# Sparse attention and MLP on one core: engine order from a list scheduler, scores in row halves, batch 1's row sums from row reads

## The chip, the cores and the metric

One core of one Trainium2 chip runs the whole program. The metric is the device time of one execution in microseconds (us). Before the change its median is 319.44 us over three runs (318.63 to 320.3).

Engines: TensorE (PE) multiplies matrices; its weight loads are listed as PEld and run beside its matmuls. VectorE (DVE), ScalarE (ACT) and GpSimd (POOL) do elementwise work; SyncE (SP) issues transfers, and so does POOL. PE writes into PSUM. Each engine works through its own list in order; an instruction that waits holds up all behind it.

## The reference: what is computed

Inputs are q, k, v of shape [4 batches, 8 heads, 768 rows, 64], and two weight matrices, 512x2048 and 2048x512.

```python
k_sum = k.reshape(B, H, nb, 32, D).max(axis=3)      # 24 blocks of 32 rows
v_sum = v.reshape(B, H, nb, 32, D).mean(axis=3)
scores_l = where(|i - j| < 16, q k^T / 8, -1e9)
scores_s = q k_sum^T / 8 + log(32)
a = softmax(concat(scores_l, scores_s))
x = a @ concat(v, v_sum)                            # heads side by side: [3072, 512]
h = x @ w_in
out = (h * clip(h + 3, 0, 6) / 6) @ w_out           # [3072, 512] float32
```

So a query row sees the 31 keys around it and the 24 block maxima.

## The kernel before

**Attention.** The unit is a pair of heads, on the upper and the lower 64 partitions. Query rows go in 12 tiles of 64. For each, `kx` holds one 128-column weight matrix: 64 keys of the tile's own, 24 block maxima (padded to 32), 16 keys of the next and 16 of the previous tile. `va` holds the matching 128 rows of values, block sums and edge rows, for both heads with a column of zeros or weights between them. A pair goes through these steps (names of the helper, line):

- `Tk`, `Tq`: PE transposes the loaded k and q into PSUM (L255 or L258, L289 or L292).
- `Tk_act` copies keys into `kx` on ACT (L263, L266); `Tk_dve` takes block maxima on DVE (L277, L279) and spreads them (L280); `edges_k` copies the edge keys (L270, L271), on ACT, DVE or POOL by batch.
- `Tq_out` copies q into `qx`, head by head (L303, L305): `qx` has 128 columns for each tile, of which each head's 64 are zero on the other head's partitions (memsets, L221). Batches 2 and 3 copy one head on DVE and one on ACT.
- `Sc`: one matmul for each tile of 64 rows, all 128 partitions and 128 columns, gives both heads' scores (L317), 4 tiles to a PSUM bank. In batches 0 and 1 (`MASK_ON_PE`) a matmul adds the mask first (L313). ACT takes the exponential (L319). Elsewhere `Mk` multiplies by the mask on DVE (L325).
- `AV`: values (L339) into `num` and `den`, one PSUM buffer each; row sums by a matmul with ones (L344), or in batches 2 and 3 from the weight column in `va`. ACT takes logarithm and exponential (L352 to L356), DVE multiplies (L365, L366, L368) into x.

**MLP.** Eight tiles of 384 rows (a batch has two). `F1` makes one of 16 column blocks of h: four matmuls (L378), Relu on ACT (L381), min and product on DVE (L382), in two PSUM buffers. `F2` sums over 16 blocks for each of three groups of 128 rows (L390); ACT copies the result out (L394) and SP stores it.

**Values.** Batches 0 and 1 read v in 128-row form (`load_vf`, L113), cast it into `va`, and form block sums on PE with an indicator matrix (`sum_pe`, L407), which DVE converts (L411) and POOL spreads (`put_sums`, L415). Batches 2 and 3 read v straight into `va` (`load_v`, L129) and again as rows of blocks (`load_vrows`, L133); `vsum` halves these five times by adds on POOL (L144), and SP sends the sums to `va` (L147). `weights_between` (L532) writes the weight column with 12 memsets. `edges_v` (L125, L126) copies edge rows by transfers on SP. Batch 3's k and q come head by head (L106), the others' pair by pair (L99). Weights load on POOL's queue (L155, L159).

**Order.** All five engines run in program order. Batch 0's first half is written out by hand. Then a work list steps through the MLP tiles in slots, each one F1 block and three F2 matmuls; `at_slot` hangs attention steps and loads on slot numbers, all chosen by hand, such as

```python
attention(1, (40, 44, 48, 51), (52, 54, 57, 60, 65, 68, 71, 74), 2, 4)
```

One slot's function issues on several engines at once, so a slot sets the place of a step in every list.

Of the kernel before, what the change touches and what calls it, by code (L numbers as in the profile page):

```python
# [8 lines left out]
F32 = mybir.dt.float32  # L9
# [16 lines left out]
NLONG = 3  # L26
MASK_ON_PE = (0, 1)
DEN_IN_VALUES = (2, 3)
BIG = 2.0 ** 33


@with_exitstack
def kernel(
# [22 lines left out]
    NM = 6  # L56
# [17 lines left out]

    qx = const.tile([128, NP, NQ, 2, QB], BF16, tag="qx", name="qx")
    at = [const.tile([128, NQ, 2, QB], BF16, tag=f"at{p}", name=f"at{p}") for p in range(NP)]
# [5 lines left out]
    kq_t, vr_t, vf_t = {}, {}, {}  # L82

    def ld_tile(name):
        return ld.tile([128, 4 * RUN * D], BF16, tag="kq", name=name, bufs=4)

    def rows_tile(t, heads, r):
        return t[0:RP].rearrange("p (h s d) -> p h s d", h=heads, d=D)[:, :, 0:r]

    def load(which, b, p, n, half=None, t=None):  # L90
        src = (k if which == "k" else q)[b, 2 * p:2 * p + 2 * n]
        if b < NLONG:
            lo, hi, r = (0, S, RUN) if half is None else (half * HALF, (half + 1) * HALF, RUN // 2)
            if t is None:
                t = rows_tile(ld_tile(which + "b"), 2 * n, r)
                i0 = 0
            else:
                t, i0 = t
            nc.gpsimd.dma_start(out=t[:, i0:i0 + 2 * n], in_=src[:, lo:hi].rearrange("h (p s) d -> p h s d", s=r))  # L99
            for i in range(n):  # L100
                kq_t[which, b, p + i, half] = t[:, i0 + 2 * i:i0 + 2 * i + 2]
        else:
            t = ld_tile(which + "b")[:, 0:n * NT * 2 * D].rearrange("p (i s j d) -> p i s j d", i=n, j=2, d=D)
            for i in range(n):
                for j in range(2):
                    nc.gpsimd.dma_start(out=t[:, i, :, j], in_=src[2 * i + j].rearrange("(s p) d -> p s d", p=128))  # L106
                kq_t[which, b, p + i, half] = t[:, i]

    def load_vf(b, p, n):

        t = vf_t[b][:, 2 * p:2 * p + 2 * n].rearrange("r h s d -> r (h s) d")
        src = v[b, 2 * p:2 * p + 2 * n].rearrange("h s d -> (h s) d")
        nc.gpsimd.dma_start(out=t, in_=src.rearrange("(s r) d -> r s d", r=128))  # L113

    def cast_v(eng, b, p, odd, lo, hi):

        t = vf_t[b][64 * odd:64 * odd + 64, 2 * p:2 * p + 2, lo:hi]
        copy = eng.copy if eng is nc.scalar else eng.tensor_copy
        copy(va[b % 2][0:QB, p, 2 * lo + odd:2 * hi:2, 0:3:2].rearrange("r t j d -> r j t d"), t)

    def edges_v(b, p0, p1, lo, hi):

        o = va[b % 2][:, p0:p1].rearrange("r p t j d -> r p t (j d)")
        a, z = max(lo, 1), min(hi, NQ - 1)
        nc.sync.dma_start(out=o[R_PREV:, :, a:hi], in_=o[QB - EDGE:QB, :, a - 1:hi - 1])  # L125
        nc.sync.dma_start(out=o[R_NEXT:R_PREV, :, lo:z], in_=o[0:EDGE, :, lo + 1:z + 1])  # L126

    def load_v(b, h):
        nc.gpsimd.dma_start(out=va[b % 2][0:QB, h // 2, :, 2 * (h % 2)], in_=v[b, h].rearrange("(t r) d -> r t d", r=QB))  # L129

    def load_vrows(b, g):
        t = ld.tile([RS, BLK, D], F32, tag="vr", name="vr")
        nc.gpsimd.dma_start(out=t[:], in_=v[b, 4 * g:4 * g + 4].rearrange("h (n t) d -> (h n) t d", n=NB))  # L133
        vr_t[b, g] = t

    def vsum(b, g):

        r = vr_t[b, g]
        n = BLK
        vs = work.tile([RS, 1, D], BF16, tag="vs", name="vs")  # L140
        while n > 1:
            n //= 2
            o = r[:, 0:n] if n > 1 else vs[:]
            nc.gpsimd.tensor_tensor(out=o, in0=r[:, 0:n], in1=r[:, n:2 * n], op=ALU.add)  # L144
        for i in range(4):
            h = 4 * g + i
            nc.sync.dma_start(out=va[b % 2][R_SUM:R_SUM + NB, h // 2, :, 2 * (h % 2)],  # L147
                              in_=vs[i * NB:(i + 1) * NB].to_broadcast([NB, NQ, D]))
# [4 lines left out]
    def load_w_in(c):  # L153
        w = d_ff // 4
        nc.gpsimd.dma_start(out=w_in_sb[:, :, c * w:(c + 1) * w], in_=w_in_v[:, :, c * w:(c + 1) * w])  # L155

    def load_w_out(c):
        w = NFT // 4
        nc.gpsimd.dma_start(out=w_out_sb[:, c * w:(c + 1) * w], in_=w_out_v[:, c * w:(c + 1) * w])  # L159
# [13 lines left out]
    def words(t):  # L173
        return t.bitcast(F32)

    vf_t[0] = gp.tile([128, H, NT, D], F32, tag="g", name="vf")

    nc.vector.memset(band[0:R_NEXT], 0.0)  # L180
    nc.vector.memset(band[R_NEXT:], -BIG)


    k0 = rows_tile(ld_tile("kb"), 4, RUN)
    q0 = rows_tile(ld_tile("qb"), 8, RUN // 2)
    k1 = rows_tile(ld_tile("kb"), 4, RUN)
    load("k", 0, 0, 1, t=(k0, 0))
    nc.gpsimd.memset(ident[:], 1.0)
    nc.gpsimd.affine_select(out=ident[:], in_=ident[:], compare_op=ALU.is_equal, fill=0.0, base=0,
                            channel_multiplier=1, pattern=[[-1, 128]])  # L190
    load("q", 0, 0, 2, 0, t=(q0, 0))
    load_vf(0, 0, 1)
    load("k", 0, 1, 1, t=(k0, 2))

# [4 lines left out]
    keep(band[0:QB], EDGE - 1, 1, -1)  # L199
    keep(band[0:QB], EDGE - 1, -1, 1)  # L200
    keep(band[R_SUM:R_NEXT], NB - 1, -1, 0)
    keep(band[R_NEXT:], EDGE, -1, 1, 0.0)
    keep(band[R_NEXT:], QB - EDGE, 1, -1, 0.0)
    nc.gpsimd.tensor_copy(maskb[:], band[:].unsqueeze(1).to_broadcast([128, NM, QB]))
    keep(maskb[R_NEXT:, 0], EDGE - 1, -1, 0)
    keep(maskb[R_NEXT:, NM - 1], -EDGE, 1, 0)
    load_vf(0, 1, 1)
    load("k", 0, 2, 2, t=(k1, 0))
    load("q", 0, 2, 2, 0, t=(q0, 4))
# [3 lines left out]
    load_w_in(1)  # L213

    nc.vector.memset(zero[:], 0.0)
    nc.vector.memset(words(kx[:, :, :, R_SUM + NB:R_NEXT]), 0.0)
    nc.vector.memset(words(kx[:, :, 0, R_PREV:]), 0.0)
    nc.vector.memset(words(kx[:, :, NQ - 1, R_NEXT:R_PREV]), 0.0)
    for h in range(2):
        for j in range(2):  # L220
            nc.vector.memset(words(qx[64 * j:64 * j + 64, :, h * NH:(h + 1) * NH, 1 - j]), 0.0)  # L221
        if h == 0:

            nc.vector.memset(ind[:], 0.0)
            for u in range(4):
                nc.vector.memset(ind[32 * u:32 * u + 32, 28 + u:29 + u], 1.0)

            nc.vector.memset(va[0][R_NEXT:, :, 0:NQ:NQ - 1].rearrange("r p t j d -> r p t (j d)").bitcast(F32), 0.0)
    nc.vector.memset(half_c[:], 0.5)
    for h in range(2):  # L230
        z = zero[:].unsqueeze(2).unsqueeze(3).to_broadcast([128, NP, NH, D // 2])
        nc.scalar.copy(words(va[0][:, :, h * NH:(h + 1) * NH, 1]), z)

    def zero_rest():
        nc.vector.tensor_scalar(mask[:], maskb[:], 1.0 / BIG, 1.0, op0=ALU.mult, op1=ALU.add)
        nc.vector.memset(ones[:, 1], 0.0)
        for i in (0, 2):
            nc.vector.memset(ones[:, i], 1.0)
            nc.vector.memset(ones[R_SUM:R_NEXT, i], float(BLK))

    def zero_va1():
        nc.gpsimd.memset(va[1][R_NEXT:, :, 0:NQ:NQ - 1].rearrange("r p t j d -> r p t (j d)").bitcast(F32), 0.0)
        nc.gpsimd.memset(words(va[1][:, :, :, 1]), 0.0)
# [4 lines left out]
    def Tk_pe(b, p):  # L248
        pool, tag = (ps_o, "o") if b == 0 else (ps_s, "s")
        tp_t["k", p] = tp = pool.tile([128, S], BF16, tag=tag, name="tpk")  # L250
        t = kq_t["k", b, p, None]
        if b < NLONG:
            for s in range(RUN):
                for j in range(2):
                    nc.tensor.transpose(tp[64 * j:64 * j + 64, s * RP:(s + 1) * RP], t[:, j, s], ident[0:RP, 0:RP])  # L255
        else:
            for s in range(NT):
                nc.tensor.transpose(tp[:, s * 128:(s + 1) * 128], t[:, s].rearrange("p h d -> p (h d)"), ident[:])  # L258

    def Tk_act(b, p):  # L260
        o, tp = kx[:, p, :, 0:QB], tp_t["k", p]
        if b < NLONG:
            nc.scalar.copy(o.rearrange("p t (c s) -> p t c s", s=RUN),  # L263
                           tp[:].rearrange("p (s t c) -> p t c s", s=RUN, t=NQ))
        else:
            nc.scalar.copy(o, tp[:].rearrange("p (t c) -> p t c", t=NQ))  # L266

    def edges_k(eng, p):
        copy = eng.copy if eng is nc.scalar else eng.tensor_copy
        copy(kx[:, p, 1:, R_PREV:], kx[:, p, 0:NQ - 1, QB - EDGE:QB])  # L270
        copy(kx[:, p, 0:NQ - 1, R_NEXT:R_PREV], kx[:, p, 1:, 0:EDGE])  # L271
# [344 lines left out]
```

## Time and profile before

| | |
|---|---|
| median of 3 runs | 319.44 us |
| profiled execution: its own time | 318.8 us |
| profiled execution: span from first to last instruction | 317.1 us |
| mean granted PE clock | 0.939 |
| busy: PE, ACT, DVE, POOL | 79%, 54%, 50%, 37% |
| chain that ended last: PE, DVE, ACT, POOL | 42%, 24%, 13%, 8% |
| read from and written to memory | 30.41 MB, 6.29 MB |

How to read it: a line of a timeline has start, duration, engine, line of the kernel, operation, out<-in and count, and in brackets how long the engine stood idle before it and what ended that. A line of waits has total, number and longest. In stages, each engine's busy time is followed by its number of instructions. PE's matmuls are pipelined, so their durations overlap; the distance from start to start is what one costs.

### The profile page before, as it was taken

Reading aid. Unit: us, or ns where it says so; the run is one execution under the profiler, and the core shown is the slowest. Engines: PE = TensorE matmul, PEld = TensorE weight load, DVE = VectorE, ACT = ScalarE, POOL = GpSimd, SP = SyncE. Lnnn points to the kernel's source line nnn. Section 1 sums busy time; section 2 is a strip of 40 time slices with the busy share of each in tenths; the row PEclk is TensorE's granted clock in tenths of the full one; section 3 lists DMA queues with packets and bytes.
Section 4 is the critical chain, followed back from the end, with each engine's and each line's share of the span. In section 5 each row is a group of like instructions: output and inputs, shape, how many; then the busy total and the mean of one; then the engine's idle time right before and its main releaser. Section 6 shows DMA issues by size and latency. Waiting matters only on the chain.

```text
span 317.1 us, 5297 instructions
## 1 busy us (share of the span) xinstructions
PE 249.5 (79%) x2035; PEld 144.2 (45%) x2060; DVE 157.6 (50%) x315; ACT 172.0 (54%) x321; POOL 117.8 (37%) x162
## 2 busy tenths in 40 slices
PE   2874879999677981759649898867849899999995
PEld 1653445566344540435425444534525445555542
DVE  6564684247677142175564656336545555444410
ACT  5454753555445661554848675545767675555521
POOL 7827960129103999470199991000000000000000
PEclk9999999999799996596998999979978999999999
DMA  6996999832245992399097913600000100110111
GB/s 108 186 211 112 194 204 233 153 107 48 40 76 91 233 99 23 44 147 70 3 117 184 99 20 45 178 2 33 36 0 0 68 0 33 55 48 33 36 66 66
DMA packets 45498, 27.75 MB, mean 88 GB/s; under 512 B 31136, under 2 KB 40736, under 8 KB 45088
## 3 DMA queue, kind: packets, MB, share of 16 engines
q0 software_dynamic: 36224, 18.35, 42.2%
q1 hardware_dynamic: 9248, 9.05, 11.1%
q8 instruction: 16, 0.26, 0.4%
q14 instruction: 10, 0.08, 0.1%
HBM read 30.41 MB, written 6.29 MB: 116 GB/s over the span
## 4 chain that ended last, share of the span: by engine, by line
PE 42%; DVE 24%; ACT 13%; POOL 8%; issue 6%; DMA 5%; SPq 0%; ACTq 0%; POOLq 0%
PE op L390 16%; PE hp L378 15%; DVE g L382 7%; ACT r L381 4%; DVE qx L303 3%; DMA va<-va 3%; PE sp L317 3%; POOL vr L144 3%; POOL va L532 3%; DVE x L366 2%; DVE red L277 2%; POOL va L129 2%; DMA out_dram<-ot 2%; PE sums L407 2%; DVE x L365 2%
## 5 line engine op out<-in xcount | busy, mean ns | idle before, releaser
L382 DVE SCALAR_TENSOR_TENSOR g<-r,hp 128x384 bf16<-128x384 f32 x128 | 69.2, 553 | 107.0 <-ACT r L381 106.0
L378 PE MATMUL hp<-x,win 128*128 128x384 bf16 x512 | 106.4, 341 | 8.9 <-DVE g L382 7.6
L390 PE MATMUL op<-wout,g 128*128 128x512 bf16 x359 | 97.6, 385 | 3.4 <-DVE g L382 1.8
L381 ACT ACTIVATE r<-hp,half_c 128x384 f32<-128x384 f32 x128 | 73.1, 580 | 43.6 <-PE hp L378 41.2
L378 PEld LDWEIGHTS <-win 128*128 128x128 bf16 x512 | 48.8, 101 | 47.5 <-issue 15.8
L390 PEld LDWEIGHTS <-g 128*128 128x128 bf16 x384 | 37.2, 99 | 36.1 <-issue 4.3
L319 ACT ACTIVATE at<-sp 128x512 bf16<-128x512 f32 (+1 forms) x52 | 27.9, 563 | 38.4 <-PE sp L317 38.3
L317 PE MATMUL sp<-qx,kx 128*128 128x128 bf16 x192 | 20.5, 240 | 15.3 <-POOL kx L271 7.9
L339 PE MATMUL num<-at,va 128*128 128x64 bf16 x288 | 14.1, 196 | 23.1 <-DVE x L368 10.0
L339 PEld LDWEIGHTS <-va 128*128 128x128 bf16 x384 | 15.5, 100 | 33.9 <-DVE x L365 11.9
L317 PEld LDWEIGHTS <-kx 128*128 128x128 bf16 x192 | 16.5, 109 | 25.6 <-issue 10.9
L303 DVE COPY qx<-tpq 64x384 bf16<-64x384 bf16 (+1 forms) x28 | 20.3, 727 | 7.4 <-PE tpq L289 7.1
L270 POOL COPY kx<-kx 128x176 bf16<-128x176 bf16 x8 | 2.7, 332 | 54.8 <-ACT kx L266 34.6
L415 POOL COPY va<-vs 32x768 bf16<-32x768 bf16 (+1 forms) x12 | 14.3, 1190 | 19.5 <-DVE vs L411 18.9
L394 ACT COPY ot<-op 128x512 f32<-128x512 f32 x24 | 13.7, 582 | 11.7 <-PE op L390 10.0
L144 POOL TENSOR_TENSOR vr<-vr 96x1024 f32<-96x1024 f32 (+3 forms) x16 | 19.1, 1194 | 1.1
L368 DVE TENSOR_TENSOR x<-num,lg 128x384 bf16<-128x384 f32 x16 | 8.9, 555 | 20.2 <-ACT lg L356 15.8
L532 POOL MEMSET va<- 32x768 bf16 (+1 forms) x24 | 17.7, 737 | 0.9
L356 ACT ACTIVATE lg<-lg 128x384 f32<-128x384 f32 x32 | 16.7, 522 | 1.0
L407 PE MATMUL sums<-vf,ind 128*32 128x128 f32 x96 | 13.7, 299 | 1.3 <-DVE qx L303 0.9
L355 ACT ACTIVATE lg<-den 128x384 f32<-128x384 f32 x16 | 7.8, 490 | 11.6 <-PE den L344 11.4
L277 DVE TENSOR_REDUCE red<-tpk 128x24 bf16<-128x768 bf16 x12 | 11.4, 954 | 5.2 <-ACT kx L263 4.9
(73 smaller groups left out, 235.6 us busy)
## 6 DMA issues: line engine op xcount, KB each, us to landing
out_dram<-ot SPq DMA_DIRECT2D x24, 256.0 KB
vr<-in_v_dram POOLq DMA_DIRECT2D x4, 768.0 KB, 9.0
win<-in_moe_w_in_dram POOLq DMA_DIRECT2D x4, 512.0 KB, 10.5
wout<-in_moe_w_out_dram POOLq DMA_DIRECT2D x4, 512.0 KB, 12.1
kb<-in_k_dram POOLq DMA_DIRECT2D x5, 384.0 KB, 5.6
qb<-in_q_dram POOLq DMA_DIRECT2D x5, 384.0 KB, 7.6
vf<-in_v_dram POOLq DMA_DIRECT2D x4, 384.0 KB, 6.5
vf<-in_v_dram POOLq DMA_DIRECT2D x2, 768.0 KB, 17.2
```

The costliest lines, as they stand in the source:

```text
L144: nc.gpsimd.tensor_tensor(out=o, in0=r[:, 0:n], in1=r[:, n:2 * n], op=ALU.add)
L277: nc.vector.tensor_reduce(red[:], tp[:].rearrange("p (s n c) -> p n s c", s=RUN, n=NB), axis=AX.XY, op=ALU.max)
L303: copy(o.rearrange("p t (c s) -> p t c s", s=r), tp[rows, 0:n].rearrange("p (s t c) -> p t c s", s=r, t=nt))
L317: nc.tensor.matmul(sp[:, i], kx[:, p, t], qx[:, p, t], start=not on_pe, stop=not on_pe or i == n - 1)
L319: nc.scalar.activation(a, sp[:, 0:n], AF.Exp, scale=scl)
L339: nc.tensor.matmul((num, den)[j * both][:, i * QB:(i + 1) * QB], w[:, j * D:j * D + 128], a[:, t, j], start=both or (i == 0 and j == 0), s ...
L378: nc.tensor.matmul(hp[:], w_in_sb[:, kt, ft * 128:(ft + 1) * 128], xt[t][:, kt], start=(kt == 0), stop=(kt == NP - 1))
L381: nc.scalar.activation(r[:], hp[:], AF.Relu, bias=half_c[:], scale=1.0 / 6.0)
L382: nc.vector.scalar_tensor_tensor(gt[t][:, ft], r[:], 1.0, hp[:], op0=ALU.min, op1=ALU.mult)
L390: nc.tensor.matmul(op[:], gt[t][:, ft, ts * 128:(ts + 1) * 128], w_out_sb[:, ft], start=(ft == 0), stop=(ft == NFT - 1))
L407: nc.tensor.matmul(sums[R_SUM:R_NEXT], ind[:, 28 - 4 * s:60 - 4 * s], vf_t[b][:, 2 * p:2 * p + 2, s], start=(s == 0), stop=(s == NT - 1))
L532: nc.gpsimd.memset(va[i][r0:r1, p, :, 1], float(w))
```

## The change

- A class `Plan` in the kernel. Each step is entered with engine, cost in us, a place (priority), what it reads and writes, the buffers it takes and a transfer time. `order` then simulates the five engines: whichever engine can start an operation first takes, of its operations ready within 0.12 us, the one with the lowest place. `run` issues all in that order. Costs are constants; transfers are modelled as one queue for POOL.
- `qx` is [128, pairs, 768], without zeros; `Tq` copies both heads at once. Scores are two matmuls for a tile, each on 64 rows, 64 columns and a PSUM bank of its own; the exponential runs by head on 384 columns.
- Masks of batch 1 move to DVE; a mask operation covers both heads of half a pair's rows.
- Batch 1's block sums come from `load_vrows` and `vsum`; `sum_pe` and `put_sums` remain for batch 0. `zero_va1` clears the sum rows as well (4 more memsets).
- `NLONG = 4`: batch 3 loads k and q as the others do, 4 transfers for 16, and transposes in 16 pieces.
- Key edges of batch 0 on DVE, its first q copies on ACT. Matmuls on zeros (`fill`) may be placed where PE would idle before 24 us of the simulated time; 14 are.
- Every F2 runs group by group; F1 of tiles 0 and 2 uses four PSUM buffers.

The core of the diff:

```diff
-NLONG = 3
-MASK_ON_PE = (0, 1)
+NLONG = 4
+MASK_ON_PE = (0,)
...
+            for e, c in cand.items():
+                t0 = max(free[e], min(x[0] for x in c))
+                p = min((x for x in c if x[0] <= t0 + self.NEAR), key=lambda x: (x[1], x[2]))
+                t = max(t0, p[0])
+                if best is None or t < best[0]:
+                    best = t, p[2]
...
-    qx = const.tile([128, NP, NQ, 2, QB], BF16, tag="qx", name="qx")
+    qx = const.tile([128, NP, S], BF16, tag="qx", name="qx")
...
-            nc.tensor.matmul(sp[:, i], kx[:, p, t], qx[:, p, t], start=not on_pe, stop=not on_pe or i == n - 1)
+            for u in range(NH):
+                t = half * NH + u
+                for j in range(2):
+                    rows = slice(64 * j, 64 * j + 64)
+                    nc.tensor.matmul(sp[j][:, u], kx[rows, p, t], qx[rows, p, t * QB:(t + 1) * QB],
+                                     start=not on_pe, stop=not on_pe or u == NH - 1)
...
+            nc.vector.tensor_tensor(a, a, msk.unsqueeze(1).to_broadcast([128, 2, NH, QB]), op=ALU.mult)
...
+        op(e, cost, put, [tq], [f"qx{p}{h}" for h in halves], tail=0.15)
...
+    def first_loads_1():
+        load("k", 1, 0, 2)
+        load("q", 1, 0, 2)
+        load_vrows(1, 0)
+        load_vrows(1, 1)
+        load("k", 1, 2, 2)
+        load("q", 1, 2, 2)
+        zero_va1()
+        load_vf(1, 0, 2)
+        load_vf(1, 2, 2)
+        vsum(1, 0)
+        vsum(1, 1)
+        for p in range(NP):
+            cast_v(nc.gpsimd, 1, p, 0, 0, 6)
+            cast_v(nc.vector, 1, p, 1, 0, 6)
+            edges_v(1, p, p + 1, 0, NQ)
...
-    attention(1, (40, 44, 48, 51), (52, 54, 57, 60, 65, 68, 71, 74), 2, 4)
+    for b in range(1, B):
+        attention(b, 48 + 32 * (b - 1))
```

## The prediction

> **What bounds the kernel now.** I read the busy table first, then the stages, the waits of TensorE (PE), and the timeline where it waits. From the page:
>
> ```profile
> span 317.1 us, 5297 instructions
> ...
> PE 249.5 (79%) x2035; PEld 144.2 (45%) x2060; DVE 157.6 (50%) x315; ACT 172.0 (54%) x321; POOL 117.8 (37%) x162
> ...
> PEclk9999999999799996596998999979978999999999
> ```
>
> PE leads, but a matmul's end is modelled, so I count PE by start-to-start time. The timeline of the last stretch, where nothing but the two MLP products runs:
>
> ```profile
> 269.10 0.81 PE L378 MATMUL hp<-x,win 128*128 128x384 bf16 x4
> 269.75 0.81 PE L390 MATMUL op<-wout,g 128*128 128x512 bf16 x2
> 270.39 0.81 PE L378 MATMUL hp<-x,win 128*128 128x384 bf16 x4
> ```
>
> Four F1 matmuls take 0.65 us, three F2 matmuls 0.65 us. Both products hold 128 such groups: 256 x 0.65 = 166.4 us. The same reading elsewhere at full clock: 16 transposes 0.46 us (155.46 to 155.92), 12 value matmuls of 64 columns 0.35 (152.99 to 153.34), the two row-sum matmuls 0.33, four scores of 128 columns 0.22, a mask matmul of 512 columns 0.22, 12 v-sum matmuls 1.43.
>
> F1 starts in earnest at 33.6 us and the last matmul ends at 313.3. In between PE has 166.4 + scores 168 x 0.055 = 9.2 + masks 3.9 + values 12 x 0.68 + 16 x 0.35 = 13.8 + transposes 11.2 + v sums 4 x 1.43 = 5.7, together 210.2 us of work in 279.7. So **69.5 us are lost**. The span is 33.6 + 210.2 + 69.5 + 3.8 (last copy and store). Stages:
>
> ```profile
> 120.00:130.00 10.00, 1.69 (x23) 1.31 (x24) 0.83 (x2) 0.20 (x1) 8.48 (x12) 0.56 0.09 15
> ...
> 230.00:240.00 10.00, 5.58 (x33) 3.13 (x33) 4.90 (x10) 5.94 (x12) 0.00 (x0) 0.69 0.00 0
> ...
> 270.00:280.00 10.00, 9.89 (x54) 5.29 (x55) 4.23 (x8) 5.08 (x9) 0.00 (x0) 1.00 0.15 55
> ```
>
> The columns are PE, its weight loads, DVE, ACT, POOL, granted clock, DMA. After 260 us nothing is lost. The loss lies where attention and MLP mix, and it comes twice, as idle time and as the half clock that follows. The waits say on what:
>
> ```profile
> PE num L339 <- DVE x L368: 10.0, 7, 3.0
> PE num L339 <- DVE x L365: 8.7, 2, 4.4
> PE sp L317 <- POOL kx L271: 7.9, 1, 7.9
> PE hp L378 <- DVE g L382: 7.6, 7, 2.5
> ```
>
> After 33.6 us PE's waits add up to about 48 us; the mean clock of 0.939 is another 0.061 x 317 = 19 us. That is the 69.5 to within 3. No engine is full: it is order.
>
> **The change, part by part.**
>
> *PE's work after F1 starts.* Masks of batch 1 leave PE (12 x 0.22 = -2.6), and its v sums (-5.7). Batch 3 is transposed in 16 pieces, not 6: 8 x (0.46 - 0.33) = +1.0. A score group is now 12 matmuls of 64 columns on half the rows; no such row exists. Above: each weight load in the open, 12 x 0.10 (the weight-load mean) = 1.2 us. Below: two halves side by side, 6 x 0.029 = 0.17. I take 0.35, the row of 12 value matmuls of 64 columns, each with its load: 28 x 0.35 = 9.8 against 9.2. Sum **203.5 us**.
>
> A row on leaving a tile shape: the transposes (96*64 in the array) start at 155.46, the full-array matmul after them at 155.92, 29 ns per piece with the change of shape inside. So I price a switch at nothing. The Trainium skill, TensorE Tiling, section Tiling Modes, Key Properties, says that changing the tiling mode drains TensorE; with two switches for each of 28 score groups at 0.17 us (an F2 matmul's 0.385 less its step of 0.216), an estimate, the total would be 10 us higher. No trace here has row halves.
>
> *The qx copy.* Now DVE copies one head's rows and ACT the other's, out of one tile, and ACT waits for DVE:
>
> ```profile
> ACT qx L303 <- DVE qx L303: 12.4, 4, 3.9
> ...
> ACT qx L305 <- DVE qx L305: 10.9, 4, 3.1
> ```
>
> Behind that ACT copy stand the Relus: at 161.39 it ends a wait of 3.86 us, and PE then stands 4.43 us until 165.34. After: one DVE copy of 128x768, taken at the 0.96 us of the 64-row copy. ACT's copy goes, 8 x 0.79. DVE gains batch 1's masks, 8 per 384-column half of both heads, 0.60 by columns from 0.43 for 512: 4.8 us beside 50% idle time. Nothing on the path.
>
> *Start.* 2.8 us of DVE memsets on qx go. The two key-edge copies of a pair go from ACT (0.34 each) to DVE (0.25). Following the new lists of instructions with rows of before: first transposes 4.9, values of pair 0 at 18 (their edge DMA took 7.8 us among loads, 11.95 to 19.78); cast of pair 3 on ACT about 22.9, its edge DMAs 1.2 + 2.6, values of pair 3 at 26.7, logarithm and exponential 1.0, x 0.56, hand-overs: F1 at **29.4** instead of 33.6. The matmuls on zeros that fill idle time before 24 us cost nothing, their cover being the waits for loads (4.9 us before the first transpose); uncovered, 14 x 0.22 = 3 us.
>
> *POOL, and a new wait.* Today batch 2's POOL list is one run, ahead of the key edges that the scores need:
>
> ```profile
> 102.58 9.22 POOL L532 MEMSET va<- 64x768 bf16 x12
> 111.76 5.99 POOL L129 DMA_DIRECT2D va<-in_v_dram  x8
> 117.81 5.01 POOL L144 TENSOR_TENSOR vr<-vr 96x1024 f32<-96x1024 f32 x4
> ...
> 128.51 0.33 POOL L270 COPY kx<-kx 128x176 bf16<-128x176 bf16 x1
> ```
>
> That is the 7.9 us wait. The new list has the edges of pairs 0 and 1 ahead of the sums; the wait goes. But batch 1's row sums now run on POOL (2 x 5.36, from 117.81 to 123.17), behind batch 2's 12 memsets and 8 v loads. And by the new program's own list of waits, each POOL transfer waits for the one eight before it: the sixth v load for the first half of batch 1's vf, the eighth for q of pairs 2 and 3. In the profile the loads are one full queue from 10 to 62 us:
>
> ```profile
> 42.21 2.88 POOL L113 DMA_DIRECT2D vf<-in_v_dram  x2
> 54.52 0.70 POOL L99 DMA_DIRECT2D qb<-in_q_dram  x1 [9.43 <-PE tpq L289]
> 58.36 0.82 POOL L119 CAST va<-vf 64x768 bf16<-64x768 f32 x1 [3.14 <-DMA vf<-in_v_dram]
> ```
>
> vf's first half lands at 58.3, its second at 62 (18.3 us after its issue). Two row loads of 768 KB now go before them, 3.2 to 3.7 us each at 210 to 240 GB/s: 64.8, 68.2, then q 70.6. So the last v load goes out at 71.4, the sums run to 82.1, the cast of pair 0 to 82.9; SP, busy until 85.1 with the last sums (4 x 0.6) and an output between them, then issues pair 0's edges, the second at 85.7, which lands 2.5 us on (25.83 to 28.38 before): **batch 1's first values at 88.2**. PE gets there at 29.4 + 44.3 (32 F1 and 20 F2 groups, 33.8; batch 0's second half 6.6; batch 1's transposes and scores 3.9) + 4 of waits = 77.7. **Stall 10.5 us**. Queued behind it on PE: the rest of F2 of tile 1 and all of F1 of tile 2. Before it was an equal wait in batch 2, after which the clock stayed at half for 5.7 us of work: 2.9 us more.
>
> *Other waits.* num and den have one buffer each, so value groups of batch 1 are 2.2 us apart (0.49 + 0.52 + 0.56 and hand-overs). The new order has the third and fourth too close and F1 right behind: 0.6 + 1.3 + 1.8 = 3.7. Of the other 40 us of PE's waits (48 less 7.9) 36 remain to place: between none and all. I take a third, 12.3, since work that is ready stands next in the new order, though it was set from fixed costs that the chip won't keep. In all 16.
>
> Batch 3's k and q in 4 transfers for 16: 10.9 us less of POOL's issue, none of it waited for.
>
> **Sum.** 29.4 + 203.5 + 16 + 10.5 + 2.9 + 3.8 = 266.1 us of span. The profiled execution took 318.8 for its 317.1, and the median is 0.6 above it: 266.1 + 1.7 + 0.6 = 268.4, **268 us**.
>
> **Rivals.**
> *The order holds, no POOL stall* (v loads don't wait for vf, or vf lands by 58): less 13.4, **255 us**. For: POOL never waited for a transfer slot in the profile. Against: its transfers never were so close behind a full queue.
> *Row halves cost more*: every weight load in the open, 28 x (1.2 - 0.35) = 24 us, **292 us**; the same if all 36 us of waits stay (+24). For: 384 small loads for 192. Against: the 0.35 row.
> *Slower: attention on ACT holds up the Relus.* F1 runs on two buffers; each Relu waits in order behind exponentials and logarithms. With 56 exponentials x 0.5, 12 x 1.0 and 16 x 1.5 for the logarithm pairs and 12 copies x 0.8, 74 us stand in front of Relus. If none is hidden under PE, it replaces the 16: 266.1 - 16 + 74 + 2.3 = **326 us**. It decides from 67 us unhidden, 0.6 us for each of the 112 F1 groups that share the time. For: the same interplay costs 48 us now. Against: ACT is 46% idle, and the copies that wait inside ACT's queue go. That the order changes nothing would look like this too, at the point of equality.
>
> **Chances.** Forecast 0.45, order without stall 0.25, dear scores or waits 0.20, ACT 0.10. A measurement tells 0.5% (1.6 us) from no change: of the last, 0.02 falls within it, 0.08 above. Faster 0.90, same 0.02, slower 0.08. The range takes in the second and third: 255 less the 7 by which waits may shrink further gives 248; to 292.
>
> **What would show it.** Right: F1 from about 29; a PE wait of 6 to 13 us before batch 1's first values, POOL's adds of batch 1 between 71 and 82; no long PE wait on POOL's key edges; scores 12 in about 0.35; no ACT wait on a DVE qx copy; 256 groups of MLP at 0.65. Wrong: POOL adds done by 70 (255); 12 scores taking over 0.8 us (292); PE waits on Relu or g beyond 40 us (slower).

## The result, and the profile after

The kernel after takes **267.77 us**, median of 4 runs (267.68 to 267.83). The kernel before, beside it on the same chip, takes 319.03 (318.16 to 320.3): a ratio of 0.839, 95% interval 0.836 to 0.8421. The forecast was 268. The total is right; several of its terms are not, and what follows is mostly about them. Here and below a median is of all executions, while a ratio leaves out those that were over 1.5% above the fastest of their kernel, so the two need not divide out.

The page of the kernel after, the same lines as of before:

```profile
span 266.0 us, 5782 instructions
...
PE 236.4 (89%) x2286; PEld 128.3 (48%) x2286; DVE 159.1 (60%) x300; ACT 165.6 (62%) x323; POOL 115.2 (43%) x160
...
PEclk9999999999997599979999999999999999999998
```

PE is busy for 89% of the span, before for 79%. The clock falls in two places only, 80 to 93 us and about 115. The first is the stall that the prediction was about. TensorE's timeline there:

```profile
77.89 0.81 PE L678 MATMUL hp<-x,win 128*128 128x384 bf16 x4 [2.42 <-DVE g L686]
...
79.76 1.46 PE L707 MATMUL op<-wout,g 128*128 128x512 bf16 x6
89.25 0.80 PE L625 MATMUL nd<-at,va 128*128 128x64 bf16 x12 [8.04 <-DMA va<-va]
89.86 0.83 PE L630 MATMUL nd<-at,ones 128*128 128x384 bf16 x2
90.49 2.76 PE L707 MATMUL op<-wout,g 128*128 128x512 bf16 x6
```

PE stands for 8.04 us ahead of batch 1's first values, for a transfer into `va`. Afterwards six F2 matmuls take 2.76 us, where six took 1.46 ahead of the stall: half clock. The waits of TensorE in the kernel after:

```profile
PE nd L625 <- DMA va<-va: 11.1, 3, 8.0
PE hp L678 <- DVE g L686: 5.1, 7, 2.4
PE sp L591 <- DVE qx L560: 1.7, 1, 1.7
PE hp L678 <- DVE x L654: 1.7, 2, 1.2
PE nd L625 <- POOL va L751: 1.6, 1, 1.6
```

Of the four rows shown of before, 7.9 on POOL's `kx` is gone, the 18.7 on `x` ahead of `num` have nearly gone (`num` and `den` are now `nd`; 0.3 are left), and 7.6 on `g` are 5.1. From F1's start to the last matmul, PE's gaps add up to 19.3 us; before, counted in the same way, to 49.1. Of the 51.1 us that the span lost, these gaps are 29.8, F1's earlier start (30.4 for 33.6) is 3.2, and 18.1 are PE's own time between them (212.5 for 230.6). The forecast's change of work accounts for 6.7 of the last; the mean clock rose from 0.939 to 0.972, but no run splits the rest. On ACT's list no wait for a `qx` copy is left; before it had two, of 12.4 and 10.9.

What stands behind the 8.04 us is on POOL's timeline:

```profile
54.90 3.76 POOL L288 DMA_DIRECT2D va<-in_v_dram  x5
60.13 0.75 POOL L288 DMA_DIRECT2D va<-in_v_dram  x1 [1.48 <-DMA vf<-in_v_dram]
63.95 0.74 POOL L288 DMA_DIRECT2D va<-in_v_dram  x1 [3.07 <-DMA vf<-in_v_dram]
65.11 0.75 POOL L288 DMA_DIRECT2D va<-in_v_dram  x1 [0.42 <-DMA stg<-in_q_dram]
65.92 5.62 POOL L307 TENSOR_TENSOR vr<-vr 96x1024 f32<-96x1024 f32 x4
```

Batch 2's v loads wait, from the sixth on, for transfers they have no data in common with, each the one eight before it. Batch 1's row sums stand behind them. The chain of what ended last goes on from there:

```profile
46.52 18.30 DMA stg<-in_q_dram
65.11 0.75 POOL va L288
65.92 2.36 POOL vr L307
...
80.81 0.80 SPq L311
81.72 0.61 SPq L278
82.38 6.74 DMA va<-va
```

So the mechanism is the forecast one, link by link: queue slot, v load, sums, SP, edges.

### The profile page after: what moved, and what is told of

It is laid out like the page before. It is cut to its first block, busy times and chain, and to the rows that moved or that the text cites. A ratio compares the mean times of both kernels' runs of the same rounds, so it can differ in the third digit from the quotient of the medians.

```text
span 266.0 us, 5782 instructions
## 1 busy us (share of the span) xinstructions
PE 236.4 (89%) x2286; PEld 128.3 (48%) x2286; DVE 159.1 (60%) x300; ACT 165.6 (62%) x323; POOL 115.2 (43%) x160
## 4 chain that ended last, share of the span: by engine, by line
PE 61%; DMA 14%; POOL 9%; ACT 5%; DVE 5%; issue 3%; SPq 2%; POOLq 0%; ACTq 0%
PE op L707 24%; PE hp L678 23%; DMA stg<-in_q_dram 8%; DMA va<-va 5%; POOL vr L307 4%; PE nd L625 3%; PE sp L591 2%; PE sums L736 2%; PE tpk L494 2%; PE tpq L550 2%; POOL va L751 2%; PE nd L630 1%; ACT r L683 1%; SPq L311 1%; POOL va L265 1%
## 5 line engine op out<-in xcount | busy, mean ns | idle before, releaser
L678 PE MATMUL hp<-x,win 128*128 128x384 bf16 x512 | 96.9, 330 | 6.8 <-DVE g L686 5.1
L683 ACT ACTIVATE r<-hp,half_c 128x384 f32<-128x384 f32 x128 | 72.2, 579 | 45.7 <-PE hp L678 41.1
L307 POOL TENSOR_TENSOR vr<-vr 96x1024 f32<-96x1024 f32 (+3 forms) x24 | 30.9, 1286 | 1.5
L595 ACT ACTIVATE at<-sp 128x384 bf16<-128x384 f32 x64 | 27.7, 487 | 4.5 <-PE sp L591 4.4
L625 PE MATMUL nd<-at,va 128*128 128x64 bf16 x384 | 16.9, 195 | 13.1 <-DMA va<-va 11.1
L654 DVE TENSOR_TENSOR x<-nd,lg 128x384 bf16<-128x384 f32 x16 | 8.9, 557 | 22.8 <-ACT lg L642 22.7
L598 DVE TENSOR_TENSOR at<-at,mask 128x768 bf16<-128x768 bf16 x24 | 18.5, 771 | 6.7 <-ACT at L595 6.5
L502 ACT COPY kx<-tpk 128x768 bf16<-128x768 bf16 x16 | 12.8, 798 | 8.3 <-PE tpk L494 8.2
L651 DVE TENSOR_TENSOR x<-nd,lg 64x384 bf16<-64x384 f32 x16 | 8.8, 547 | 12.6 <-ACT lg L642 11.6
L560 DVE COPY qx<-tpq 128x768 bf16<-128x768 bf16 (+1 forms) x16 | 13.6, 849 | 3.5 <-PE tpq L550 3.5
L288 POOL DMA_DIRECT2D va<-in_v_dram x16 | 12.0, 765 | 5.0 <-DMA vf<-in_v_dram 4.5
## 6 DMA issues: line engine op xcount, KB each, us to landing
vf<-in_v_dram POOLq DMA_DIRECT2D x2, 768.0 KB, 18.7
```

The costliest lines, as they stand in the source:

```text
L595: nc.scalar.activation(a[:, j], sp_t[keys[j]][:], AF.Exp, scale=scl)
L598: nc.vector.tensor_tensor(a, a, msk.unsqueeze(1).to_broadcast([128, 2, NH, QB]), op=ALU.mult)
L625: nc.tensor.matmul((num, den)[j * two][:, u * QB:(u + 1) * QB], w[:, j * D:j * D + 128], a[:, j, t], start=two or (u == 0 and j == 0), sto ...
L678: nc.tensor.matmul(hp[:], w_in_sb[:, kt, ft * 128:(ft + 1) * 128], xt[t][:, kt], start=(kt == 0), stop=(kt == NP - 1))
L683: nc.scalar.activation(r[:], c[0][:], AF.Relu, bias=half_c[:], scale=1.0 / 6.0)
```

## Experiments

Ratios are to the kernel before on the same chip (319.5 to 321.7 us there). Chips differ by more than 1 us, so kernels compared with the kernel after are read by both time and ratio.

**1. The parts without the scheduler.** Steps are issued in order of their place numbers; the 14 matmuls on zeros are left out.

```diff
-        for i in self.order():
-            self.ops[i]["fn"]()
+        for o in sorted(self.ops, key=lambda o: (o["place"], o["i"])):
+            if not o.get("spare"):
+                o["fn"]()
```

> The changed kernel with every operation as it is, issued in the order of its place number and not as the list scheduler would have it; the matmuls on zeros are left out. If the scheduler's order makes the gain: near the kernel before, 300 to 320 us, with PE waits spread over attention steps. If the changed operations make it (qx copied once, masks and sums off PE, scores in row halves): under 280 us.

Measured: 364.24 us (362.1 to 366.75), ratio 1.1333 (1.1264 to 1.1402). A miss on both sides. TensorE's waits of this kernel:

```profile
PE nd L626 <- DMA va<-va: 62.6, 5, 27.3
PE hp L679 <- DVE g L687: 18.7, 12, 11.7
```

The place numbers are priorities to choose by, not an order. It follows that the parts alone gain nothing without a fitting order; it does not follow that they would lose in one made by hand for them.

**2. Batch 1's sums ahead of batch 2's v loads.** In the planner, batch 2's v loads follow batch 1's last addition.

```diff
-        plan.add("POOL", 0.8, place(), issue, (), ...
+        plan.add("POOL", 0.8, place(), issue, ["vr11"] if b == 2 else (), ...
```

> Batch 2's eight v loads may start only after batch 1's last POOL add. If the 8.0 us wait before batch 1's first values comes from the adds standing behind v loads that wait for transfer slots: the wait is gone or under 2 us, and with it 2.3 us of half clock: 256 to 259 us. If the edge transfers themselves or the full load queue set that time: 266 us or more.

Measured: 259.81 us (256.26 to 262.03), ratio 0.8018 (0.7949 to 0.8087). The time is the theory's (256 us by ratio); the wait is shorter, but not under 2 us. POOL and TensorE of this kernel:

```profile
55.03 5.03 POOL L307 TENSOR_TENSOR vr<-vr 96x1024 f32<-96x1024 f32 x4
```

```profile
77.63 1.46 PE L707 MATMUL op<-wout,g 128*128 128x512 bf16 x6
81.99 0.80 PE L625 MATMUL nd<-at,va 128*128 128x64 bf16 x12 [2.90 <-DMA va<-va]
82.60 0.83 PE L630 MATMUL nd<-at,ones 128*128 128x384 bf16 x2
83.22 2.27 PE L707 MATMUL op<-wout,g 128*128 128x512 bf16 x6
```

The sums start 10.9 us earlier (55.03 for 65.92) and the wait is 2.90 us for 8.04. That is 5.1 us; PE's waits for `g`, which are 5.1 us in the kernel after, are 0.7 here, so not all of the gain is the stall.

**3. A planner that knows the eight slots.** A POOL transfer may start only when the one eight before it has landed.

```diff
+                if o["eng"] == "POOL" and o["dma"] and len(lanes) >= 8:
+                    t = max(t, lanes[-8] + self.CROSS)
```

> The scheduler's model lets a POOL transfer start only when the one eight before it has landed; nothing else is changed. If the unmodelled slot wait is the cause of the stall, the new order avoids it: 254 to 259 us. If not: 264 to 270 us.

Measured: 259.87 us (256.64 to 261.34), ratio 0.805 (0.7987 to 0.8114). Told of the slots, the planner finds an order as good as experiment 2's. The wait ahead of batch 1's first values is 2.80 us.

**4. Batch 1's sums back on TensorE**, as before: no row loads and no additions for batch 1.

```diff
-        load_vrows(1, 0)
-        load_vrows(1, 1)
...
-        vsum(1, 0)
-        vsum(1, 1)
+            sum_v(p, 1)
+            put_sums(p, 0, 1)
+            put_sums(p, 1, 1)
```

> Batch 1's block sums go back to PE (indicator matmuls, DVE conversion, POOL spread), without batch 1's row loads and adds. Theory that POOL's adds cost the stall (8.0 + 2.3 us) and hold DVE up between 66 and 78 us (3.6 us of PE waits on g): gains 13.9, pays 5.7 of PE: about 260 us. Rival, that the row reads are a gain as such: 270 us or more (5.7 us of PE and POOL's spreads come on top).

Measured: 260.36 us (258.68 to 261.8), ratio 0.8082 (0.8024 to 0.8139). Here PE doesn't wait ahead of batch 1's first values. The row reads with their additions cost about 7 us by time, 10 by ratio, as they were placed; well placed (3) they are neither gain nor loss against the sums on TensorE. One term of the theory did not come: PE's waits for `g` are 5.5 us, not less than the 5.1 of the kernel after, for one of 3.89 came up elsewhere (shown at the end).

**5. Both of 3 and 4.** 

> The kernel after, with both edits that each took out the stall before batch 1's first values: batch 1's row sums on TensorE, and a planner that starts a POOL transfer only when the one eight before it has landed. Alone 260.4 and 259.9 us. The stall can go only once: 256 to 261 if it is one and the same; under 254 if the planner's lanes also mend the later waits.

Measured: 260.97 us (259.39 to 261.67), ratio 0.8171 (0.8123 to 0.8219). Nothing is added (by ratio the two together are, if anything, slower than either): it is one stall.

**6. Batch 2's loads behind batch 1's edges.** The k, q, row and v loads of batch 2 follow, in the planner, the last edge transfer of batch 1.

```diff
+            ... ["va13e0"] if b == 2 else () ...
```

> As a_vsum_first, and all of batch 2's loads (k, q, v and rows) may be issued only after batch 1's last edge transfer is issued; k and q buffers are given out in order of place. There batch 1's edges took until 81.9 to land after an issue at 76.3, beside k, q and row loads. Theory that those loads hold the small transfers up: edges land within 3 us, PE's waits for va transfers in that stretch fall from 5 to under 2 us: 2 to 5 us less than a_vsum_first. Rival, that the small transfers are slow by themselves or that batch 2's late loads make a new wait: no gain, or slower.

Measured: 278.72 us (274.99 to 281.87), ratio 0.8611 (0.854 to 0.8682). The rival holds. The entry binds the plan alone: on the chip POOL issued k and q at 70.4, ahead of the edges at 77.2, so it was no clean test of the landing. The edges then took 5.07 us. What it did is visible in its chain, in batch 2:

```profile
117.79 0.72 POOL vr L307
...
123.17 0.67 SPq L278
123.84 0.05 issue
123.89 16.73 DMA va<-va
140.62 0.14 issue
140.76 0.80 PE nd L625 x12
```

Batch 2's sums end at 119 us. Between 119.65 and 129.4 POOL issues a load of k, one of q, two row loads of 768 KB and two of v, and the edge transfer issued at 123.89 lands 16.73 us later. PE waits 21.13 us for it.

**7. Key edges on VectorE, in the kernel before.**

```diff
-        eng = nc.vector if b == 1 else nc.gpsimd
+        eng = nc.vector
```

> The kernel before, with the key edges of batches 2 and 3 copied on DVE and not on POOL: nothing else. Theory that its 7.9 us wait and 2.9 us of half clock came only from the edges' place behind POOL's list: about 309 us, ratio 0.967. Rival, that the next operand (batch 2's sums and edge rows, also behind POOL's list) is late right after: under 4 us gained.

Measured: 312.39 us (308.46 to 314.56), ratio 0.965 (0.9578 to 0.9722). As expected by ratio.

**8. Both query copies on VectorE, in the kernel before.**

```diff
-nc.scalar.copy if b > 1 else nc.vector.tensor_copy
+nc.vector.tensor_copy
```

> The kernel before, with both heads' q copies of batches 2 and 3 on DVE, so that no ACT copy waits for DVE in front of Relus. Theory that this wait (23.3 us of ACT idle, 8.7 us of PE behind one chain) costs: 4 to 9 us faster. Rival, that DVE's chain (0.56 to 0.96 us longer for each pair) takes its place: within 2 us of before.

Measured: 309.42 us (308.01 to 310.38), ratio 0.963 (0.9586 to 0.9675): right in direction and somewhat more than expected. The two waits of ACT for VectorE's `qx` are gone from its list, and PE's wait of 8.7 us for `x` ahead of `num` is 4.1.

**9. Both edits of 7 and 8.** 

> The kernel before, with both one-line edits: key edges of batches 2 and 3 on VectorE, and both copies of the queries of batches 2 and 3 on VectorE. Alone they gave 312.4 us (0.965) and 309.4 (0.963). If the two waits are apart, the gains add: about 299 us, ratio 0.93. If they lie behind each other in the same chain or VectorE becomes the wait, less: 304 to 310. Either way most of the 51 us to the kernel after is left to the order.

Measured: 305.09 us (303.46 to 306.24), ratio 0.9564 (0.9497 to 0.9632). Not additive: 0.965 x 0.963 would be 0.929. POOL's wait is gone, but PE now waits 7.8 us for VectorE's `qx`. Two lines give 14 us of the 51. That most of the rest needs the new order is argued from experiment 1; the other parts of the change were not tried in the old order.

**10. Each score matmul of batches 1 to 3 twice.** The scores of batches 1 to 3 are formed twice over.

```diff
-                for j in range(2):
+                for j in (0, 1) if on_pe else (0, 1, 0, 1):
```

> The changed kernel with each score matmul of batches 1 to 3 issued twice (24 groups of 24 instead of 12; the second overwrites the first with the same values). A group takes 0.28 us of PE. If PE is the bound where the scores stand: 24 x 0.28 = 6.7 us more, about 274 us. If they stand in PE's waits: less than 3 us more.

Measured: 270.68 us (269.32 to 272.59), ratio 0.8428 (0.8371 to 0.8486). TensorE of the kernel after, then of this one:

```profile
65.81 0.35 PE L591 MATMUL sp<-qx,kx 64*128 64x64 bf16 x12
66.10 1.47 PE L678 MATMUL hp<-x,win 128*128 128x384 bf16 x8
```

```profile
68.67 0.53 PE L591 MATMUL sp<-qx,kx 64*128 64x64 bf16 x24
69.12 1.47 PE L678 MATMUL hp<-x,win 128*128 128x384 bf16 x8
```

12 take 0.28 us from start to start, 24 take 0.45: 0.17 for twelve more, 14 ns each, and 0.11 for the group. So 24 groups gained 4.1 us of PE work, not the 6.7 that 0.28 for each would make; 1.2 (by ratio) to 2.9 us (by time) of it came through, the former within the noise.

**11. One row half after the other.** The loops over tile and head change places.

> The kernel after, with the 12 score matmuls of a group in another order: the six of one head (one row half of the array), then the six of the other, where the kernel alternates. Theory: what alternation buys is that neighbours in different halves run beside each other. 24 matmuls of a group took 0.45 us and 12 took 0.28, so 14 ns each beside about 0.11 for the group; a single one of 64 columns at the rate of F1 (384 columns in 0.1625 us) takes 27 ns. Without neighbours in other halves a group takes 0.11 + 12 x 0.027 = 0.43 us, 28 groups 4.2 us more TensorE work, of which waits swallow the part that lies before the stall: 269 to 272 us. Rival: the hardware overlaps them in either order, or the group's time is set by its weight loads: 0.28 us and 267.8 as before.

Measured: 269.15 us (268.53 to 270.25), ratio 0.8438 (0.8395 to 0.848). A group in this kernel:

```profile
67.74 0.42 PE L591 MATMUL sp<-qx,kx 64*128 64x64 bf16 x12
68.10 1.47 PE L678 MATMUL hp<-x,win 128*128 128x384 bf16 x8
```

0.36 us (0.355), between the theory's 0.43 and the rival's 0.28. Alternating the halves is worth 0.07 us a group, about 2 us in all of PE work; the two kernels' times, 1.4 us apart, are not clear of noise by ratio.

**12. Short additions.** Each row sum's wide additions on POOL are cut into pieces of 256 columns.

```diff
+            for a in range(0, n, 4):
+                e = min(n, a + 4)
+                nc.gpsimd.tensor_tensor(out=o[:, a:e], in0=r[:, a:e], in1=r[:, n + a:n + e], op=ALU.add)
```

> The kernel after, with the two wide additions of each row sum on POOL cut into pieces of 256 columns (4 and 2 pieces for one of 1024 and one of 512); what is computed is the same. In the kernel after, each VectorE copy or mask that runs 0.9 us or more over its usual time ends within about 0.4 us of the end of a POOL addition that runs beside it (mask 0.56 becomes 1.5 to 2.3 us, copy of 288 columns 0.3 becomes 1.6 to 2.1). Theory, VectorE waits until POOL's current instruction ends: with pieces of about 0.6 us the longest mask falls to under 1.3 us, the longest such copy to under 1.0, the sum of the excess from 9.9 us to under 4. The time hardly moves, 266 to 269 us, since the wait of TensorE before batch 1's first values ends with a transfer behind POOL, which has some 0.5 us more of work for each sum. Rival, the two engines share bandwidth and both are slowed in proportion: the excess stays at 8 to 10 us and the masks beside the sums at 1.5 to 2.3.

Measured: 265.15 us (264.27 to 266.18), ratio 0.831 (0.8268 to 0.8351). The longest mask fell from 2.26 to 0.99 us and the longest copy of 288 columns from 2.07 to 0.67, as the theory has it; the excess, which is the time over the median of the same form, fell from 9.9 to 3.8 us counted over instructions that ran at least 0.2 us over, and from 10.8 to 5.0 counted over all, since short waits are left and a piece takes 0.78 us, not 0.6. The time fell a little below the 266 to 269 expected. VectorE and POOL in the kernel after, and last the longest mask of this one:

```profile
110.14 2.07 DVE L518 COPY kx<-red 128x288 bf16<-128x288 bf16 x1
142.37 2.26 DVE L598 TENSOR_TENSOR at<-at,mask 128x768 bf16<-128x768 bf16 x1 [0.21 <-ACT at L595]
```

```profile
109.77 5.01 POOL L307 TENSOR_TENSOR vr<-vr 96x1024 f32<-96x1024 f32 x4
141.86 5.00 POOL L307 TENSOR_TENSOR vr<-vr 96x1024 f32<-96x1024 f32 x3
```

```profile
142.83 0.99 DVE L600 TENSOR_TENSOR at<-at,mask 128x768 bf16<-128x768 bf16 x1
```

The first addition of the group at 141.86 ends at 144.21, and the mask, undisturbed 0.56 us, at 144.63. The copy (median 0.30) that starts at 110.14 beside the addition from 109.77 to 112.12 ends at 112.21. The seven VectorE instructions with the largest excess end 0.09 to 0.43 us after the end of a POOL addition.

## Why the prediction was right, and where it was not

The sum against the trace, by its own terms: F1's start 29.4 and 30.4; PE's work and the half clock 203.5 + 2.9 = 206.4 and 212.5; idle 10.5 + 16 = 26.5 and 19.3; the tail 3.8 and 3.8. Off by +1.0, +6.1 and -7.2: the total is as close as it is because these cancel.

- **The stall** (10.5 by forecast, 8.04) is the mechanism named. Getting the sums out from behind the slot waits cut it to 2.90 and 2.80 us (2, 3), taking them off POOL removed it (4), and both together gained no more (5): shown. The forecast's sizes were off, and offset each other. The transfers in front landed about 5 us earlier than summed (the last v load goes out at 65.1, not 71.4), and POOL's additions end at 77.7, not 82.1. By ratio experiments 2 to 4 come to 256 to 258 us, about the 255 of the rival without a stall.
- **"which lands 2.5 us on"** failed. It took 6.74 us. 2.5 was the row of a quiet stretch, while the same text used 7.8 for such a transfer among loads; the DMA share from 80 to 90 us is 0.98. POOL issues five loads of batch 2 from 81.07 to 84.15, around it. Experiment 6's 16.73 us beside loads points the same way. Experiment 5's trace has both cases: the edges of batch 1's first two pairs, among POOL's loads, land 2.8 to 4.3 us after their issue, and the four of the last two pairs, issued from 71.29 to 73.96 with no POOL packet on the DMAs, after 2.24 to 2.33. So loads beside it, not the transfer itself, make it late. The DMA queues (packets, MB, share), first of the kernel after from 82.38 to 89.12, then of experiment 5 from 71.29 to 76.28, where q0 is POOL's and has no row, and q1 is SP's:

```profile
q0 software_dynamic: 956, 0.95, 92.5%
q1 hardware_dynamic: 351, 0.34, 17.6%
```

```profile
q1 hardware_dynamic: 272, 0.53, 46.1%
```

- **PE's arrival at 77.7** was 81.2. F1's start accounts for 1.0; waits up to there were 5.2, not 4; and 17 shape switches 1.6 (below).
- **"I price a switch at nothing"** failed, by a misread row. The 0.46 us of 16 transposes holds the way out of a shape; the way in sits in the matmul ahead. From its start to the next group's, the last F1 matmul takes 257 ns ahead of a score group and 256 ahead of transposes, where ahead of F2 or values it takes 162; the last F2 312 or 309, against 216. In the kernel before, F1 ahead of transposes took 255 already, and ahead of its full-array scores 163. So entering costs 94 ns, 52 times after F1's start: 4.9 us. On the way out, the last score of a group takes 122 ns to the next group; within it, starts come mostly in pairs 3 or 4 ns apart, with 25 to 37 ns from pair to pair. The Trainium skill, TensorEngine Tiling (Array Packing), Tiling Modes, Key Properties, says that a change of tiling mode drains TensorE; the trace agrees, and has a smaller price than the 0.17 us put in then.
- **The score group**, 0.35: 0.28 measured, with 0.094 on entry 0.37. The size was right for wrong reasons: matmuls side by side are cheaper (14 ns, not 29), switches dearer. The rival of dear row halves is out (0.28, not 1.2), and what row halves bring is not PE time: 28 groups x 0.37 = 10.5 us, against 9.2 before. What they brought, the query copy without zeros, ended a wait that experiment 8, which ends it by another edit, prices at about 12 us in the old order.
- **DVE's masks "beside 50% idle time"**: wrong. Masks, casts and copies were held by POOL's additions, 9.9 us of excess in all (1.5 before, by the same count), and PE waited for `g` behind them (2.42 us at 77.89, 1.14 at 71.87). With short additions the excess shrank and 1% of the time went (12): so much is shown. By which of PE's waits is argued: those for `g` fell from 5.1 to 2.5 us and the 1.7 for `qx` went, but `g` has only 2.3 in experiment 10 too, with long additions. PE's gaps came to 13.3 us, 6.0 less, of which 2.6 show in the time, as F1 started 1.0 us later in that trace and PE's own work took 2.5 more.
- **Other waits, 16**: 11.2. I had kept a third of the old waits; less stayed.
- **The half clock**, 2.9: about 4, worked out from the half-speed groups after 89 us and about 115 us. With the switches and the cheaper scores, 203.5 - 2.0 + 4.9 + 4 = 210.4; 2.1 us of the 212.5 are not placed.
- **ACT in front of the Relus** (the slower rival) did not come: ACT's row of waits for F1 is 41.1 us, before 41.2, and PE never waited for ACT's Relu by itself.
- **The fills "cost nothing"** was not tried by itself, nor were batch 1's masks back on PE.

## What to carry to other kernels

A list scheduler is only as good as its model: it left 8 us here to a limit on transfers in flight and to an engine held by another, and a few lines for the eight slots got the 8 us back. A shape switch, or any cost paid at a boundary, should be read on both sides, in the start-to-start distance of the group before as well as the group's own. A transfer priced by its quietest row is priced too low when the same step of the plan issues bulk loads beside it.

## What the runs showed of the hardware that was not expected

- **VectorE's masks, copies and casts waited until POOL's current addition ended.** A mask went from 0.56 to 2.26 us, a copy from 0.30 to 2.07; with pieces a third as long, to 0.99 and 0.67. The min and product from PSUM (0.55 us, 17 times) and one reduction (0.95) ran unchanged beside the same additions. The Trainium skill, SBUF — State Buffer, Who interferes with whom, says that copies and casts in a two-port mode, and a tensor_tensor with both inputs in SBUF, contend with GpSimd for a port pair that is held for a whole instruction. The trace agrees in the times (the ends 0.09 to 0.43 us behind POOL's); ports it doesn't show.
- **In one place it held through POOL's transfer issues too.** In experiment 4 a copy of 288 columns lasted through three v loads' issue and an addition, and PE waited behind it. VectorE and then TensorE of that kernel:

```profile
119.81 4.41 DVE L518 COPY kx<-red 128x288 bf16<-128x288 bf16 x1
```

```profile
124.68 1.44 PE L678 MATMUL hp<-x,win 128*128 128x384 bf16 x4 [3.89 <-DVE g L686]
```

- **Matmuls in two row halves run side by side**: 14 ns for one of 64 columns when halves alternate, about half of the 27 ns that 64 columns take at F1's rate (162.5 ns for 384), and the two of a pair start 3 or 4 ns apart. Six of one half in a row, then six of the other, take 0.07 us more a group (11).
